# Bias rows shared with GpSimd as maxima, a two-product maximum as MLP activation, six of eight half batches turned by DMA, and a new issue order

## The chip, the cores and the metric

One core of one Trainium2 chip runs the kernel. Its engines are TensorE (PE for the matrix products, PEld for the loading of their stationary operand), VectorE (DVE), ScalarE (ACT), GpSimd (POOL) and SyncE (SP, which here only issues DMAs). The metric is the device time of one execution in microseconds, as the median of several executions.

## The reference, cut to what matters

```
# q, k, v: (4 batches, 8 heads, 576 positions, 64); hidden = 32; d_model 512; d_ff 2048
scores = q @ k^T / 8
psi_rel = log1p(|i - j|); psi_i = log1p(max(i, 1)); x = psi_rel / psi_i
h = max(x * w1 + b1, 0)            # 32 numbers for each pair (i, j)
bias = h @ w2                      # one number for each head and pair (i, j)
attn = softmax(scores + bias)      # with 1e-9 added to the sum
y = attn @ v                       # heads side by side: 2304 tokens x 512
h = y @ w_in                       # 2304 x 2048
g = max(h, 0) + alpha * min(h, 0)
out = g @ w_out                    # 2304 x 512
```

The weights of the MLP arrive as 64-bit floats and are put together from their two halves on the chip.

## The kernel before, in words

There is one program of some 14,700 instructions. Every step is recorded first as an operation with a sort key and a nominal duration (`Planner.op`), and some operations may run on either of two engines. `Planner.plan` then lays all of them out as a list schedule, from the table `ORDER` (a key for each part, offsets, and prices for the second engine of a choice), and the instructions are issued in that order on each engine. Each engine then runs its own list strictly in order, and semaphores hold it where an operand is missing. So the table, the nominal durations and the rules of the planner set what stands behind what on each engine and on SP's DMA queue.

The parts are these.

- **Bias net** (`bias_tile`, 36 tiles of 16 positions). A tile takes four *bias rows*: 128 partitions (4 positions x 32 hidden units) by 576, max(R + PSI, 0), each made by ACT (L473) or DVE (L470). PE multiplies the four by `w2b` (L482), ACT or DVE scales the result out of PSUM (L488, L491), and a DMA stores it in a scratch tensor in HBM.
- **MLP weights** (`weights`, 8 pieces `fp`). DVE puts the 64-bit numbers together (L650, L653: three instructions for 512 columns), the largest magnitude is found, ACT or POOL makes a rounded f16 half (L666, L667), and DVE the remainder in f16 (L393). The products then take three f16 passes in place of one in f32.
- **Queries and keys** (`qk_turn`). PE turns them (L560). Batch 0 keeps them in f32; batches 1 to 3 split them into two f16 halves.
- **Attention** (`unit`). Batch, half of the heads (`hf`, 4 heads), head pair and range of rows make a unit; a half batch is four units, two for rows 0 to 255 and two for rows 256 to 575. A unit works through *tiles* of 128 rows of one head (in the longer range one more tile holds the last 64 rows of both heads): scores on PE (L585 or L586), bias added and the maximum taken on DVE (L766), exponential and its sum on ACT (L769), sum plus 1e-9 and reciprocal on DVE (L772 or L774, L776). What follows has two forms, and `by_dma(b, hf)` chooses between them. In the f32 form POOL scales the tile by the reciprocal (L791), PE turns it in five 128 x 128 pieces (L800), ACT or DVE copies it out of PSUM (L810, L811), and PE multiplies by V in f32 (L829). In the DMA form POOL or ACT writes a scaled f16 half into a buffer `a16` (L781, L782), DVE writes the remainder beside it (L784), SP issues DMA transposes of the buffer (L787; the tile of 64 + 64 rows takes two), and PE multiplies by V in f16, three passes (L821). There are two `a16` buffers. The half batches (1,1), (2,0), (2,1) and (3,1) take the DMA form.
- **MLP** (`chunk`, 9 chunks of 256 tokens; `layer_pair`, 8 per chunk). PE makes 2 x 128 hidden units (L896, 24 matmuls) into the only buffer `H` in PSUM. ACT takes the positive and the negative part (L902, L903), DVE joins them with alpha (L905, twice), ACT or DVE rounds to f16 (L909), DVE or POOL makes the remainder (L910, L911), and PE adds into `O` (L917, 12 matmuls). A chunk needs all eight heads of its tokens.

```
def by_dma(b, hf):
    return (b, hf) in [tuple(i) for i in o_("dma", ((1, 1), (2, 0), (2, 1), (3, 1)))]
...
pl.op([("ACT", 790, on_act)] + [("DVE", 560, on_dve)], key, [t_R, t_T], [hb], tag="H")
...
A(lambda: nc.scalar.activation(g.t, hv(), AF.Relu, scale=sp), 700, ky, [hb, t_sig], [g])
A(lambda: nc.scalar.activation(nn.t, hv(), AF.Relu, scale=npt), 700, ky, [hb, t_sig], [nn])
```

## Time and profile before

| what | value |
|---|---|
| time, three runs | 746.77, 747.82 (median), 749.71 us |
| the profiled execution's own time | 744.54 us |
| its span, first to last instruction | 742.8 us |
| PE, DVE, ACT, POOL busy, share of the span | 93%, 70%, 60%, 16% |
| 16 DMA engines, SP's queue | 61.5% of their span |
| mean granted clock of TensorE | 0.992 |

The span is the time from the first instruction of any engine to the end of the last one; 1.7 us of the execution lie outside it. A busy share is an average over stages that differ: the first 161.5 us hold the bias net, the weights and the first attention of batch 0, the last 96.5 us the MLP alone.

### The profile page before, as it was taken

To read this page: it belongs to the slowest core of one execution; us is meant where nothing else is said; L and a number is where in the kernel's file an instruction comes from. 1 tells how busy PE (TensorE), PEld (TensorE's weight loads), DVE (VectorE), ACT (ScalarE), POOL (GpSimd) and SP (SyncE) were. 2 spreads that over 40 slices of the span, in tenths; PEclk is the share of its full clock that TensorE was granted. 3 is DMA by queue.
4 is the path that set the end of the run, shared out by engine and by line. 5 is a ranking of instruction groups with operands and counts; after the bars stand their busy time and mean duration, and the time that the engine had idled before them with its cause. 6 is when DMAs were issued, how large, how long until landed. Compare 5 with 4: busy or idle time off the path is not lost.

```text
span 742.8 us, 14670 instructions
## 1 busy us (share of the span) xinstructions
PE 687.5 (93%) x5425; PEld 429.9 (58%) x5425; DVE 521.3 (70%) x1281; ACT 447.0 (60%) x826; POOL 117.2 (16%) x149
## 2 busy tenths in 40 slices
PE   4888777689999989999999999999999999999997
PEld 1333333357566746665566666665686566666663
DVE  6898989898878877778678777666377666334342
ACT  5888988877655756666455666655576454132322
POOL 0000222323322222122011111122120011000000
PEclk9998999999999999999999999999999999999999
DMA  7999876525458256989898977966435867000000
GB/s 199 248 275 354 326 236 225 185 97 157 120 158 206 63 146 145 191 176 216 185 172 167 226 151 164 200 124 111 141 105 148 157 149 128 1 29 1 29 1 28
DMA packets 180998, 114.04 MB, mean 154 GB/s; under 512 B 157504, under 2 KB 157504, under 8 KB 180928
## 3 DMA queue, kind: packets, MB, share of 16 engines
q1 hardware_dynamic: 178624, 113.11, 61.5%
q8 instruction: 42, 0.69, 0.4%
q10 hardware_dynamic: 2304, 0.01, 0.2%
q14 instruction: 28, 0.23, 0.1%
HBM read 74.16 MB, written 15.34 MB: 120 GB/s over the span
## 4 chain that ended last, share of the span: by engine, by line
PE 62%; DMA 1%; DVE 1%; ACT 1%; issue 0%; SPq 0%; ACTq 0%; DVEq 0%
PE O L917 23%; PE H L896 22%; PE S L586 5%; PE A L821 4%; PE A L829 2%; PE S L800 2%; PE S L560 2%; DMA fg<-scr 1%; DVE fg L766 1%; PE O L800 0%; PE O L586 0%; ACT mg L877 0%; DMA out_dram<-mg 0%; PE A L455 0%; ACT fg L769 0%
## 5 line engine op out<-in xcount | busy, mean ns | idle before, releaser
L896 PE MATMUL H<-x,win 128*128 128x256 f16 x1728 | 200.7, 273 | 1.2 <-ACT mg L903 1.1
L917 PE MATMUL O<-wout,mg 128*128 128x512 f16 x864 | 199.1, 380 | 1.5 <-ACT at L810 0.8
L896 PEld LDWEIGHTS <-win 128*128 128x128 f16 x1728 | 166.9, 98 | 33.5 <-issue 7.2
L917 PEld LDWEIGHTS <-mg 128*128 128x128 f16 x864 | 81.6, 98 | 93.6 <-issue 5.7
L769 ACT ACTIVATE fg<-fg,st 128x576 f32<-128x576 f32 x144 | 110.3, 767 | 42.2 <-DVE st L766 38.6
L902 ACT ACTIVATE mg<-H,sm 128x512 f32<-128x512 f32 x72 | 49.4, 686 | 135.3 <-PE H L896 124.4
L905 DVE SCALAR_TENSOR_TENSOR mg<-mg,sm 128x256 f32<-128x256 f32 x144 | 68.5, 504 | 84.2 <-ACT mg L903 84.2
L766 DVE CUSTOM_DVE_ANT_0 fg<-S,fg 128x576 f32<-128x576 f32 x128 | 93.7, 751 | 33.6 <-PE S L586 29.3
L791 POOL TENSOR_SCALAR fg<-fg,st 128x576 f32<-128x576 f32 x72 | 62.5, 880 | 174.1 <-DVE st L776 61.8
L482 PE MATMUL S<-at,w2b 128*32 128x512 f32 (+1 forms) x448 | 63.1, 462 | 21.0 <-DVE at L470 10.2
L781 POOL TENSOR_SCALAR a<-fg,st 128x576 f16<-128x576 f32 x40 | 33.5, 838 | 221.9 <-DMA at<-a 51.1
L473 ACT ACTIVATE at<-cst 128x576 f32<-128x576 f32 x89 | 63.7, 765 | 5.7 <-DVE cst L433 5.7
L784 DVE SCALAR_TENSOR_TENSOR a<-fg,st,a 128x576 f16<-128x576 f32 x72 | 60.4, 844 | 4.0 <-POOL a L781 2.8
L482 PEld LDWEIGHTS S<-at,w2b 128*32 128x32 f32 x448 | 23.3, 117 | 60.1 <-issue 17.3
L586 PE MATMUL S<-qk 64*128 64x288 f16 (+1 forms) x654 | 51.3, 285 | 3.2 <-DVE st L766 2.4
L800 PE MATMUL S<-cst,fg 128*128 128x128 f32 x290 | 41.1, 281 | 9.7 <-POOL fg L791 7.0
L910 DVE TENSOR_TENSOR mg<-mg 128x512 f16<-128x512 f32 x68 | 47.2, 694 | 3.7 <-ACT mg L909 2.3
L903 ACT ACTIVATE mg<-H,sm 128x512 f32<-128x512 f32 x72 | 48.9, 680 | 0.1
L586 PEld LDWEIGHTS <-qk 64*128 64x128 f16 (+1 forms) x720 | 31.8, 97 | 25.9 <-issue 20.7
L829 PE MATMUL A<-at,five 128*64 128x320 f32 (+3 forms) x320 | 44.9, 415 | 0.6 <-DVE at L811 0.6
L800 PEld LDWEIGHTS S<-cst,fg 128*128 128x128 f32 x290 | 32.1, 142 | 17.3 <-POOL fg L791 8.5
L821 PE MATMUL A<-at,five 128*64 128x256 f16 (+3 forms) x480 | 34.3, 288 | 0.0
(136 smaller groups left out, 777.5 us busy)
## 6 DMA issues: line engine op xcount, KB each, us to landing
fg<-scr SPq DMA_DIRECT2D x64, 576.0 KB, 4.6
scr<-fg SPq DMA_DIRECT2D x36, 288.0 KB, 3.8
mg<-in_moe_w_in_dram SPq DMA_DIRECT2D x13, 512.0 KB, 5.5
mg<-in_moe_w_out_dram SPq DMA_DIRECT2D x12, 512.0 KB, 6.3
fg<-scr SPq DMA_DIRECT2D x32, 144.0 KB, 4.6
out_dram<-mg SPq DMA_DIRECT2D x18, 256.0 KB, 2.4
five<-in_q_dram SPq DMA_DIRECT2D x32, 128.0 KB, 4.0
five<-in_k_dram SPq DMA_DIRECT2D x32, 128.0 KB, 3.4
```

What stands on the lines that cost most here:

```text
L473: nc.scalar.activation(hb.t, R[:, lo:lo + S], AF.Relu, bias=PSI[:, g:g + 1], scale=1.0)
L482: nc.tensor.matmul(ps.t[32 * gl:32 * gl + 32, c:n], lhsT=w2b, rhs=hs[gl].t[:, c:n], start=True, stop=True)
L586: return [(lambda a, dst=dst, zq=zq, zk=zk, i=i: nc.tensor.matmul(dst(a), lhsT=tr16(qt)[at, 0, pr, zq, lo:lo + n], rhs=tr16(qt)[at, 1, pr, ...
L766: V(lambda x=x, sl=sl, st=st, ls=ls: nc.vector.tensor_tensor_reduce(out=in_halves(ls[x]()), in0=halves(sl[x].t), in1=in_halves(ls[x]()), s ...
L769: A(lambda x=x, st=st, ls=ls: nc.scalar.activation(ls[x](), ls[x](), AF.Exp, bias=st.t[:, x:x + 1], scale=-1.0, accum_out=st.t[:, 2 + x:3 ...
L784: V(lambda x=x, rec=rec, ls=ls, a16=a16: nc.vector.scalar_tensor_tensor(a16.t[:, 640:640 + S], ls[x](), rec(), a16.t[:, 0:S], op0=ALU.mult ...
L791: pl.op([("POOL", 850, lambda x=x, st=st, ls=ls: nc.gpsimd.tensor_scalar(ls[x](), ls[x](), st.t[:, 6 + x:7 + x], 1.0, op0=ALU.mult, op1=AL ...
L800: nc.tensor.transpose(t5()[:, c], ls[x]()[:, lo:lo + P], EYE)
L821: nc.tensor.matmul(ps.t[64 * hh:64 * hh + 64, 0:w], lhsT=v5[0:hi, zv, n, 2 * pr + hh, :], rhs=at16(at)[0:hi, 5 * za + n, 320 * hh:320 * hh ...
L896: nc.tensor.matmul(hb.t[:, f, :], lhsT=win[:, fp, zw, kb, P * f:P * f + P], rhs=x[:, zx, kb, :], start=(n == 0), stop=(n == 11))
L905: V(lambda f=f: nc.vector.scalar_tensor_tensor(g.t[:, 256 * f:256 * f + 256], nn.t[:, 256 * f:256 * f + 256], nal[:, 2 * fp + f:2 * fp + f ...
L917: nc.tensor.matmul(ob.t[:, t, :], lhsT=gg.t[:, zg, f, P * t:P * t + P], rhs=wout[:, fp, zw, f, :], start=(first and f == 0 and (zg, zw) == ...
```

## The change

Six edits come together.

1. A bias row may also be made by POOL, as max(R, -PSI), which is the old row less PSI. What is missing, w2b times PSI, is one number for each partition of the result, and is added when the tile leaves PSUM (`shift`, from a table `MASK` that is filled once, by a small product `beta_mm`). The chosen rows in the built program: 54 on ACT, 8 on DVE, 82 on POOL (before: 101, 43, 0).
2. The MLP's activation is the maximum of two products, both read from `H` in PSUM: ACT writes h times `cu`, DVE takes the maximum of that and h times `cs`, in two halves of 256 columns. Where alpha is over 1 the signs of `cs`, `cu` and of that row of w_out are turned, so w_out is scaled in two halves.
3. `by_dma` names six half batches: (1,0) and (3,0) are added.
4. The sum plus 1e-9 is one two-step instruction on DVE or POOL (63 of 80 on POOL).
5. The buffers `a16` are handed out in the order of the program.
6. The planner's nominal durations and the whole table `ORDER` are new.

```diff
-        return (b, hf) in [tuple(i) for i in o_("dma", ((1, 1), (2, 0), (2, 1), (3, 1)))]
+        return (b, hf) in [tuple(i) for i in o_("dma", ((1, 0), (1, 1), (2, 0), (2, 1), (3, 0), (3, 1)))]
...
+            def on_pool(g=g, hb=hb, lo=lo):
+                nc.gpsimd.tensor_scalar(hb.t, R[:, lo:lo + S], 3.0e38, npsi[:, g:g + 1], op0=ALU.min, op1=ALU.max)
+
+            made.append(pl.op([("ACT", 766, on_act), ("DVE", 532, on_dve), ("POOL", 840, on_pool)], key, [t_R, t_T, t_N], [hb], tag="H"))
...
+        def shift():
+            m = sum(1 << gl for gl in range(4) if made[gl].eng == "POOL")
+            return MASK[:, m:m + 1]
...
-            nc.scalar.activation(ev.t, ps.t[:, 0:S], AF.Copy, scale=EVI[:, t:t + 1])
+            nc.scalar.activation(ev.t, ps.t[:, 0:S], AF.Identity, scale=EVI[:, t:t + 1], bias=shift())
...
+                for f in range(2):
+                    sf = so[:, f:f + 1]
+                    on_act = lambda f=f, vw=vw, dst=dst, sf=sf: nc.scalar.activation(dst(0)[:, f], vw()[:, f], AF.Copy, scale=sf)
+                    on_pool = lambda f=f, vw=vw, dst=dst, sf=sf: nc.gpsimd.tensor_scalar(dst(0)[:, f], vw()[:, f], sf, 1.0, op0=ALU.mult, op1=ALU.mult)
...
-            V(add, 190, ky, [(st, 2 + x) for x in range(n)] + [t_eps], [(st, 4)])
+            pl.op([(nm, d, lambda e=e, st=st, n=n, up=up: e.tensor_scalar(st.t[:, 4:4 + n], st.t[:, 2:2 + n], 1e-9, up, op0=ALU.add, op1=ALU.mult))
+                   for nm, d, e in (("DVE", 175, nc.vector), ("POOL", 250, nc.gpsimd))], ky, [(st, 2 + x) for x in range(n)], [(st, 4)], tag="ep")
...
-        A(lambda: nc.scalar.activation(g.t, hv(), AF.Relu, scale=sp), 700, ky, [hb, t_sig], [g])
-        A(lambda: nc.scalar.activation(nn.t, hv(), AF.Relu, scale=npt), 700, ky, [hb, t_sig], [nn])
+            A(lambda f=f: nc.scalar.activation(gf(f), hb.t[:, f, :], AF.Copy, scale=cu[:, f:f + 1]), 455, ky, [hb, t_sig], [(g, f)])
+            V(lambda f=f: nc.vector.scalar_tensor_tensor(gf(f), hb.t[:, f, :], cs[:, f:f + 1], gf(f), op0=ALU.mult, op1=ALU.max),
+              475, ky, [hb, t_sig, (g, f)], [(g, f)])
...
-    "queued": 11774.3,
+    "share": 0.984,
+    "queued": 1592841.1,
```

On DVE the program now starts with the weights. These are its rows from the fourth on, before the change: the first numbers of the bias net (L427 to L434: w1, b1 and R, PSI, w2b) stand first, then two bias rows (L470).

```order
L414 MEMSET a_86 128x640
L414 MEMSET a_87 128x640
L427 TENSOR_REDUCE sm<-sm 128x1
L428 TENSOR_SCALAR sm<-sm 128x1
L429 RECIPROCAL sm<-sm 128x1
L430 TENSOR_TENSOR sm<-sm 128x1
L431 TENSOR_TENSOR sm<-sm 128x1
L432 TENSOR_SCALAR cst<-cst,sm 128x1148
L433 TENSOR_SCALAR cst<-cst,sm 128x144
L434 TENSOR_SCALAR w2b<-w2b,sm 128x32
L470 TENSOR_SCALAR at_84<-cst 128x576 x2
```

And DVE's rows of the same place in the changed kernel, where L669 and L672 put the weights together and L428 is the first row of the bias net.

```order
L416 MEMSET a_87 128x640
L416 MEMSET a_88 128x640
L669 TENSOR_SCALAR win<-mg 128x512
L672 SCALAR_TENSOR_TENSOR win<-mg,win 128x512 x2
L669 TENSOR_SCALAR win<-mg 128x512
L672 SCALAR_TENSOR_TENSOR win<-mg,win 128x512
L669 TENSOR_SCALAR wout<-mg 128x512
L672 SCALAR_TENSOR_TENSOR win<-mg,win 128x512
L672 SCALAR_TENSOR_TENSOR wout<-mg,wout 128x512
L669 TENSOR_SCALAR wout<-mg 128x512
L672 SCALAR_TENSOR_TENSOR wout<-mg,wout 128x512 x2
L676 TENSOR_REDUCE sm<-win 128x1
```

So the twelve weight instructions have moved ahead of the numbers that every bias row waits for. On POOL the bias net of the changed kernel looks as follows (L488 is a bias row, L692 and L698 are the rounded halves of the weights; `at_85` and `fg` hold bias rows).

```order
L698 TENSOR_SCALAR win<-win,sm 128x1024
L488 TENSOR_SCALAR at_85<-cst,npsi 128x576 x2
L692 TENSOR_SCALAR wout<-wout,sm 128x512
L488 TENSOR_SCALAR at_85<-cst,npsi 128x576 x13
L530 MEMSET five_78 64x256
L488 TENSOR_SCALAR at_85<-cst,npsi 128x576 x2
L698 TENSOR_SCALAR win<-five_79,sm 128x1024
L488 TENSOR_SCALAR at_85<-cst,npsi 128x576 x12
```

Before the change POOL had only the weights and the scaling of batch 0's tiles there; now 82 bias rows stand among them. On SP, where the first half batch of batch 1 is worked, the queue before the change holds loads alone (L739 and L752 read the bias back, L507 loads q, k and v).

```order
L739 DMA fg<-scr_105 128x1152
L507 DMA five_79<-in_q_dram 128x4x64
L507 DMA five_79<-in_q_dram 64x4x64
L739 DMA fg<-scr_105 128x1152
L752 DMA fg<-scr_106 64x576 x2
L739 DMA fg<-scr_105 128x1152 x2
L752 DMA fg<-scr_106 64x576 x2
```

The changed kernel has the transposes (L818) of that half batch among the same loads (L772, L785 and L526).

```order
L772 DMA fg<-scr_105 128x1152
L818 DMA_TRANSPOSE at_85<-a_87 128x10x128
L818 DMA_TRANSPOSE at_85<-a_88 128x10x128
L772 DMA fg<-scr_106 128x1152
L818 DMA_TRANSPOSE at_85<-a_87 128x10x128
L818 DMA_TRANSPOSE at_85<-a_88 128x10x128
L772 DMA fg<-scr_106 128x1152
L785 DMA fg<-scr_107 64x576 x2
L526 DMA five_77<-in_q_dram 128x4x64 x3
L818 DMA_TRANSPOSE at_84<-a_87 128x10x128
L818 DMA_TRANSPOSE at_84<-a_88 128x10x128
```

What moved is the turning of two half batches, from PE to this queue: 40 transposes more in the program, 120 in place of 80, and 180 PE matmuls of L800 fewer, 180 in place of 360.

## Rows read from the trace of the kernel before

**Rows 1.** The page, busy time, share of the span and instructions of each engine.
```profile
PE 687.5 (93%) x5425; PEld 429.9 (58%) x5425; DVE 521.3 (70%) x1281; ACT 447.0 (60%) x826; POOL 117.2 (16%) x149
```

**Rows 2.** Busy us by stretch: length, each engine (instructions), clock, DMA share, GB/s.
```profile
0.00:161.50 161.50, 118.70 (x888) 57.28 (x888) 138.44 (x326) 134.70 (x216) 29.49 (x35) 0.97 0.77 243
161.50:646.30 484.80, 477.32 (x3934) 312.83 (x3925) 350.26 (x890) 287.82 (x570) 87.69 (x114) 1.00 0.69 151
338.00:484.00 146.00, 144.09 (x1218) 92.76 (x1217) 110.05 (x276) 92.36 (x185) 22.56 (x28) 1.00 0.90 183
508.00:564.00 56.00, 55.96 (x514) 39.02 (x512) 35.18 (x90) 34.72 (x71) 11.89 (x16) 1.00 0.39 100
646.30:742.80 96.50, 91.48 (x616) 59.80 (x612) 32.56 (x66) 24.52 (x40) 0.00 (x0) 0.99 0.05 17
```

**Rows 3.** PE's waits in the first 161.5 us: us in total, times, longest.
```profile
PE S L482 <- DVE at L470: 10.2, 2, 9.5
PE S L482 <- ACT fg L488: 9.7, 12, 1.4
```

**Rows 4.** The chain that ended last, late stretches: start us, us, what.
```profile
386.21 2.28 PE A L821 x30
...
420.41 1.88 PE A L821 x30
...
525.83 2.46 PE A L829 x20
...
551.83 0.55 PE O L800 x5
...
553.02 0.74 PE S L800 x5
...
561.37 2.99 PE A L829 x20
...
572.35 2.70 PE O L917 x12
```

**Rows 5.** Instructions of a line: ns minimum/median/maximum, first and last start.
```profile
L470 DVE TENSOR_SCALAR at<-cst x41: 487/512/1290, 8.9 to 156.1; 128x576 f32<-128x576 f32 x41
L473 ACT ACTIVATE at<-cst x89: 759/765/777, 8.9 to 157.6; 128x576 f32<-128x576 f32 x89
L791 POOL TENSOR_SCALAR fg<-fg,st x72: 737/746/1705, 88.4 to 554.1; 128x576 f32<-128x576 f32 x72
L393 DVE SCALAR_TENSOR_TENSOR win<-win,sm x4: 1276/1278/1285, 30.3 to 126.9; 128x1024 f16<-128x1024 f32 x4
```

**Rows 6.** Timeline around 136 us, POOL and DVE: start us, us, what.
```profile
136.09 2.42 POOL L791 TENSOR_SCALAR fg<-fg,st 128x576 f32<-128x576 f32 x2
136.14 1.76 DVE L393 SCALAR_TENSOR_TENSOR win<-five,sm,win 128x1024 f16<-128x1024 f32 x1 [0.94 <-POOL win L667]
137.82 1.76 DVE L393 SCALAR_TENSOR_TENSOR wout<-five,sm,wout 128x1024 f16<-128x1024 f32 x1
```

**Rows 7.** Groups by form: busy us, mean ns, then idle before and its releaser.
```profile
L902 ACT ACTIVATE mg<-H,sm 128x512 f32<-128x512 f32 x72 | 49.4, 686 | 135.3 <-PE H L896 124.4 <-issue 4.9 <-DVE a L784 4.0
L905 DVE SCALAR_TENSOR_TENSOR mg<-mg,sm 128x256 f32<-128x256 f32 x144 | 68.5, 504 | 84.2 <-ACT mg L903 84.2
L849 DVE SCALAR_TENSOR_TENSOR x<-A,sm,x 128x256 f16<-128x256 f32 x10 | 4.8, 478 | 4.5 <-ACT x L847 4.5
L847 ACT ACTIVATE x<-A,sm 128x256 f16<-128x256 f32 x10 | 4.7, 470 | 5.6 <-PE A L829 5.6
```

**Rows 8.** The transposes of 338 to 484 us, their landing, the remainder, batch 1's first scores.
```profile
L787 SPq DMA_TRANSPOSE at<-a x40: 1207/1348/2508, 338.8 to 479.4; - x40
...
DMA to landing us min/median/max: 2.9/3.5/6.3
...
L784 DVE SCALAR_TENSOR_TENSOR a<-fg,st,a x72: 792/812/1717, 282.0 to 626.6; 128x576 f16<-128x576 f32 x72
...
L586 PE MATMUL S<-qk x654: 279/283/308, 224.8 to 615.5; 64*128 64x288 f16 x140, 64*64 64x288 f16 x24
```

More of the change, by code (lines that the diff above doesn't have):

```diff
@@ L434, in attention_then_moe, with beta_mm @@
     V(lambda: nc.vector.tensor_scalar(w2b, w2b, aw, None, op0=ALU.mult), SMALL, KEY0, [t_aw, t_w2], [t_w2])
-    V(lambda: nc.vector.tensor_scalar(nal, al, -1.0, None, op0=ALU.mult), SMALL, KEY0 + 500, [t_al], [t_nal])
+    V(lambda: nc.vector.tensor_scalar(sgn, al, 1.0, -2.0, op0=ALU.is_gt, op1=ALU.mult), SMALL, KEY0 + 500, [t_al], [t_nal])
+    V(lambda: nc.vector.tensor_scalar(sgn, sgn, 1.0, None, op0=ALU.add), SMALL, KEY0 + 500, [t_nal], [t_nal])
+    V(lambda: nc.vector.tensor_scalar(npsi, PSI, -1.0, None, op0=ALU.mult), dve2(NG), KEY0, [t_T], [t_N])
+    bps, beta, t_beta = Buf(cA), cols(1), ["beta"]
+    def beta_mm():
+        for gl in range(4):
+            nc.tensor.matmul(bps.t[32 * gl:32 * gl + 32, 0:1], lhsT=w2b, rhs=tb, start=True, stop=True)
+    PE(beta_mm, 300, KEY0, [t_w2, t_tb], [bps])
+    V(lambda: nc.vector.tensor_copy(beta, bps.t[:, 0:1]), SMALL, KEY0, [bps], [t_beta])
+    V(lambda: nc.vector.tensor_scalar(MASK, MASK, beta, None, op0=ALU.mult), SMALL, KEY0, [t_beta, t_c], [t_beta])
     def p2(ar, n, guard, key, tok):
@@ L884, in chunk, with layer_pair @@
             tt = 2 * c + t
-            DMA(lambda e, t=t, tt=tt: e.dma_start(out=out[tt * P:tt * P + P, :], in_=o[t].t), P * DM * 4, key + 0.02, [o[t]], [("out", tt)])
-    def layer_pair(c, fp, ob, first, last, sp, npt, t_sig, ky):
+            DMA(lambda e, t=t, tt=tt: e.dma_start(out=out[tt * P:tt * P + P, :], in_=o[t].t), P * DM * 3.4, key + 0.02, [o[t]], [("out", tt)])
+    def layer_pair(c, fp, ob, first, last, cs, cu, t_sig, ky):
         hb = Buf(cH)
```

126 lines of the change are left out of this document (65 added, 61 removed), and 34 rows, old and new, of the table ORDER.

## Prediction

> **What bounds the kernel now.** I read the page's busy shares first, to see which engine could be the bound at all: PE, with 687.5 of 742.8 us [rows 1]. Then I cut the span into stretches, because PE idles in one of them only: of the 55.3 us that it idles, 42.8 lie in the first 161.5 us and 7.5 in the 484.8 us after them [rows 2]. So there are two kernels in one. Up to 161.5 us PE waits; its longest waits there are for bias rows from DVE and for tiles that ACT scales [rows 3], and DVE and ACT are busy for 138.4 and 134.7 us of the stretch [rows 2]. After it PE is the bound nearly everywhere, and what counts is how long PE's own instructions take; I took those from the chain that ended last, in late stretches where PE never stops. The last view was the DMA side, since the change moves work there: between 338 and 484 us, full of transposes, the DMA share is 0.90, and between 508 and 564 us, without any, 0.39 [rows 2, 8].
>
> **PE's work: -28.6 us.** Each of the two half batches that change form is four units, two with 4 turned tiles and two with 5, so 36 turns of five matmuls go. In the chain a turn costs PE 0.55 us when another follows and 0.74 us at its longest [rows 4]; I take 0.65 between them: 36 x 0.65 = 23.4 us (19.8 to 26.6). The product with V goes from f32 to three f16 passes: 2.99 us become 2.28 in the units of 320 rows, and 2.46 become 1.88 in those of 256 [rows 4]. Four units of each kind give 4 x 0.71 + 4 x 0.58 = 5.2 us. Both sit where PE is full, so their whole length should come off, if what they are exchanged for keeps up.
>
> **The first stretch: -7 us.** Of 144 bias rows ACT loses 47, at 0.765 us 36 us of work, and DVE loses 35, at 0.512 us 17.9 us; POOL gets 82, at 0.746 us, the median of its nearest row L791, 61 us [rows 5]. POOL is busy for 29.5 of the 161.5 us [rows 2], so it has the room. DVE does not gain all of its 17.9: ahead of its first MLP row the new order puts five more softmax rows (some 0.8 us each, as the remainder rows, which also go over 576 columns [rows 8]), the remainders of two more weight blocks (1.28 each for 1024 columns [rows 5]) and two remainders of V that stood later (1280 columns, by the same row 1.6 each). That is some 10 us back, so DVE gains about 8.
>
> Against that stands contention. At 136 us POOL had two L791 rows to run while DVE ran two L393 rows: DVE's took 1.76 us each and not 1.28, POOL's pair 2.42 us and not 1.49 [rows 5, 6]. So each side lost about half a microsecond for each row that met the other. The Trainium skill (SBUF — State Buffer, "SBUF: two separate sides") says why this can be: VectorE and GpSimd share one pair of SBUF ports, a lock that one holds for a whole instruction, when the VectorE operation runs in a two-port mode or reads two SBUF tensors; the trace agrees in kind, and by that rule each of the 82 rows can stop DVE. From the rows: 82 x 0.48 = 39 us of DVE time if every one meets such a row, nothing if none does. The merging and splitting of weights is about half of DVE's work ahead of the MLP, and a meeting doesn't always cost the whole 0.48, so I take 15 us. DVE's work is then 7 us longer than before, against 23 us in which it now idles and the 36 us taken from ACT, part of which DVE waits for through PE. I make the stretch 2 us shorter (bounds: 25 shorter if the rows never meet, 15 longer if they meet in most cases). In the new order PE does 12 more score matmuls, two turns and a few small ones before its first MLP matmul, some 5 us. PE's idle time there falls by 2 + 5 = 7.
>
> The start is inside this: twelve weight instructions now stand ahead of the chain w1, R, w2b on DVE, so the first bias rows move from 8.9 us [rows 5] to some 14 us, and ACT, which begins with them, idles for these 5 us more; DVE does in that time what it would have done later.
>
> **Edits that I cost at nothing.** The activation: ACT's two rows of 0.686 become two of about 0.47 (the nearest row that reads 128x256 from PSUM), DVE's two of 0.504 become two of about 0.478 [rows 7]. That takes some 31 us from ACT and 4 from DVE, but PE doesn't wait for either in the MLP. Buffer H is held for 2 x 0.686 = 1.37 us before, and for 0.47 + 2 x 0.478 = 1.43 after; the 12 matmuls into O that lie between two fillings, 2.70 us [rows 4], cover both. Without that cover it would cost 0.06 us in each of 72 pairs, 4 us. The halves of w_out, the split sum of 1e-9 on POOL and the order of `a16` are instructions of engines that PE is not waiting for. The 1e-9 on POOL stands behind POOL's longer rows and holds the reciprocal on DVE; the other tile of the unit covers it, and without that it is up to 0.75 us in a tile's chain.
>
> **The denser transposes: +9 us.** The stretch from 338 to 484 us holds 40 transposes, those of four pairs of units, in 36.5 us a pair, of which the DMA engines are busy for 0.90 x 36.5 = 32.9 [rows 2, 8]. Set against the share of 0.39 without transposes, one of them takes (0.90 - 0.39) x 146 / 40 = 1.9 us of all DMA engines, so the 40 more add about 75 us to the DMA's work and 12 pairs in a row follow each other instead of 6, a pause and 2. Batch 1 began its scores at 224.8 us [rows 8]; with 2 us off the first stretch and 5 us less PE work between, that is some 217. With the tail of 96.5 us [rows 2] as before, a span of 716 leaves (716 - 217 - 96.5) / 12 = 33.5 us for a pair. The DMA needs 32.9 of them. It fits, narrowly. Two `a16` buffers also fit: rounded half 0.77 (as ACT's rows of 576), remainder 0.81, landing 3.5 [rows 5, 8], 5.1 us for each buffer and 2.6 for a tile, 23 us for the nine tiles of a pair; with the longest landing of 6.3 it would be 35. So there is no slack left for a clump of loads, and I let PE's idle time of 7.5 us in this part more than double, by 9 (bounds: 0 and 35, the latter with a pair at 36.5, the pace of before).
>
> **Sum.** 744.5 - 28.6 - 7 + 9 = 717.9 us for an execution like the profiled one. That one lies 3.3 us under the median of the runs shown, so I forecast 721.
>
> **The rivals.** (A) The forecast, PE's work comes off and little else changes: 721, its own range 710 to 733, chance 0.52. (B) Bias rows and weights do not meet much, and the first stretch shortens by the 25 us of its bound in place of 2: 721 - 23 = 698. For it: ACT and DVE lose 54 us between them. Against it: DVE was the fuller of the two and meets POOL more often. Chance 0.14. (C) The ports decide the first stretch, 15 us longer in place of 2 shorter: 721 + 17 = 738. For it: rows 6; against it: DVE's softmax rows, reductions and copies out of PSUM stand among the weights there too, and the trace shows no such row stretched beside POOL. Chance 0.13. The rule of the Trainium skill above (SBUF — State Buffer, "SBUF: two separate sides") is this rival's mechanism. (D) The transposes are the new bound. SP's queue is one list, the two `a16` buffers a ring, and ACT, which makes more of the rounded halves now (65 against 32), stands still when a buffer is not free, with exponentials behind it. The point from which it decides: at 33.5 us a pair PE is still the bound; at 36 us a pair the span is 217 + 12 x 36 + 96.5 = 745.5 and the change is worth nothing; at 38 us it is 769.5, some 774 as a median. For it: the DMA share. Against it: the pace of before was set by PE, which was busy for 144 of the 146 us. Chance 0.15, in two thirds of it slower. (E) The exchange saves PE little, since turns run while PE would wait anyway: about 745, chance 0.06; rows 2 speak against it, as PE hardly waits where they stand.
>
> **How the numbers follow.** A to C and a part of D lie under 744; what a measurement of this kernel can tell from no change is about 0.5%, 3.7 us. Faster: 0.52 + 0.14 + 0.13 and 0.04 of D and E, 0.83. Same: 0.06. Slower: 0.11, all D. The range leaves out the lower half of B and D's slow part: 700 to 745.
>
> **What would show it.** Right: PE busy near 659 us, 180 matmuls of the turn's line, PE idle about 36 us before its first MLP matmul and 15 to 20 up to the last product with V; POOL rows of the bias net at 0.75 us alone and over 1 us beside weight rows; transposes landing in 3.5 to 5 us. Wrong: PE idle for more than 40 us in the middle with ACT or POOL waiting for DMA (D), or a first MLP matmul before 145 us (B) or after 172 (C).

## The result, and the profile after

The changed kernel takes 755.8 us (median of 4 runs, 754.1 to 758.1) against 747.8 us (746.8 to 749.7) for the kernel before on the same chip: a ratio of 1.011, 95% interval 1.007 to 1.014. It is slower, where 721 us had been forecast. The profiled execution took 755.0 us.

The page's busy time of each engine, after (before: [rows 1]):

```profile
PE 679.5 (90%) x5333; PEld 412.4 (55%) x5333; DVE 532.5 (71%) x1232; ACT 399.6 (53%) x794; POOL 201.4 (27%) x269
```

PE is down by 8.0 us and not by 28.6, and its idle time, span less busy, went from 55.3 to 73.7 us. The stretches say where. After, busy time by stretch, columns as in [rows 2]: up to the first bias matmul, the bias net, from its last matmul to the first MLP matmul, from there to the last product with V, and the tail:

```profile
0.00:22.40 22.40, 6.77 (x21) 3.67 (x21) 14.79 (x36) 4.74 (x7) 1.67 (x6) 1.00 0.79 205
22.40:155.00 132.60, 95.44 (x666) 34.65 (x667) 108.39 (x204) 80.48 (x120) 110.15 (x106) 0.95 0.74 234
155.00:195.50 40.50, 36.24 (x252) 22.20 (x249) 35.83 (x105) 29.27 (x57) 20.53 (x29) 0.96 0.47 142
195.50:660.80 465.30, 454.42 (x3814) 294.47 (x3811) 341.01 (x823) 267.29 (x570) 69.07 (x129) 0.99 0.86 178
660.80:753.20 92.40, 86.67 (x594) 57.36 (x588) 32.47 (x66) 17.85 (x40) 0.00 (x0) 0.99 0.05 18
```

Two things are to be seen. From the first MLP matmul on little is lost: PE idles 10.9 us up to the last product with V, with the DMA engines busy for 0.86 of the time. The loss lies ahead of it: the first MLP matmul comes at 195.5 us, 34.0 us later than before [rows 2]. And in the bias net POOL, with 110.2 of 132.6 us, is now the busiest engine, with DVE close behind it.

The first MLP matmul is not the same point of the work in every kernel, so below I also use the first score matmul of batch 1, when all of batch 0 has its scores. Before it comes at 224.8 us [rows 8], after 6 MLP pairs; after, at 246.3 us, after 5 (a pair is (200.7 + 199.2) / 72 = 5.6 us of PE). The prediction had put it at 217. The 29.3 us between, and the pair, are 34.9 of the 37.1 us by which the profiled 755.0 us exceed the forecast's sum of 717.9. From there to the end: before 517.9 us, after 506.9, so 16.6 us came off with the pair counted, where 28.6 - 9 = 19.6 were forecast.

What the rows on GpSimd look like. Lines of POOL and DVE in the groups view after (columns as in [rows 7]):

```profile
L488 POOL TENSOR_SCALAR at<-cst,npsi 128x576 f32<-128x576 f32 x78 | 87.3, 1129 | 38.3 <-DVE npsi L438 18.0 <-PE S L497 12.4 <-PE O L497 6.6
...
L672 DVE SCALAR_TENSOR_TENSOR five<-mg,five 128x512 int32<-128x512 int32 x24 | 21.5, 926 | 0.0
...
L672 DVE SCALAR_TENSOR_TENSOR win<-mg,win 128x512 int32<-128x512 int32 x8 | 5.5, 685 | 0.1
...
L669 DVE TENSOR_SCALAR five<-mg 128x512 int32<-128x512 int32 x12 | 7.2, 616 | 0.0
```

A row takes 1.13 us in the mean and not the 0.746 of its model [rows 5]. One and the same merging instruction of the weights, L672, takes 0.685 us in the one group and 0.926 in the other. The timeline shows how both come about (start us, us, what; POOL, then DVE):

```profile
44.75 2.94 POOL L488 TENSOR_SCALAR at<-cst,npsi 128x576 f32<-128x576 f32 x2 [0.47 <-PE S L497]
49.00 1.46 POOL L488 TENSOR_SCALAR at<-cst,npsi 128x576 f32<-128x576 f32 x2 [1.30 <-PE S L497]
85.00 1.82 POOL L488 TENSOR_SCALAR at<-cst,npsi 128x576 f32<-128x576 f32 x1
...
45.41 3.42 DVE L672 SCALAR_TENSOR_TENSOR five<-mg,five 128x512 int32<-128x512 int32 x4
48.76 1.20 DVE L676 TENSOR_REDUCE sm<-five 128x1 f32<-128x1024 f32 x1
49.89 0.88 DVE L482 TENSOR_SCALAR at<-cst 128x576 f32<-128x576 f32 x1
...
84.94 0.75 DVE L394 SCALAR_TENSOR_TENSOR wout<-wout,sm 128x512 f16<-128x512 f32 x1 [0.51 <-POOL wout L692]
85.61 0.69 DVE L672 SCALAR_TENSOR_TENSOR win<-mg,win 128x512 int32<-128x512 int32 x1
86.21 0.89 DVE L669 TENSOR_SCALAR win<-mg 128x512 int32<-128x512 int32 x1
```

At 49.0 us two rows take 0.73 us each, the first of them wholly beside a reduction; the second meets DVE's own bias row L482, and that one takes 0.88 us and not 0.51 [rows 5]. At 44.75 two run beside four mergings: 1.47 us each, and the four lose 0.7 us together. The row at 85.0 finds the remainder L394 under way, then a merging, and ends 0.5 us after the merging, at 86.82; L669, which had begun meanwhile and takes 0.42 us elsewhere, takes 0.89 and ends behind the row. So, by these records, an instruction waits for the other engine's to end, and a row can wait for two in turn. Of the 82 rows, the 17 that meet neither L672 nor L394 nor one of the one-input instructions L669 and L482 take 0.733 to 0.746 us; the 61 that meet L672 or L394 take 1.26 us in the mean. The Trainium skill (SBUF — State Buffer, "SBUF: two separate sides") has this as an exclusive lock on a shared port pair, held for a whole instruction; the trace agrees, with the 1.82 us.

Who waits for whom in the bias net, after (us in total, times, longest):

```profile
PEld S L497 <- POOL at L488: 42.3, 40, 2.3
ACT fg L507 <- PE S L497: 40.4, 26, 3.6
...
PE S L497 <- POOL at L488: 14.8, 18, 1.4
```

PE waits for GpSimd's rows, and ACT, which scales the finished tiles, for PE. In part the wait is mutual: by the line of L488 above, GpSimd itself waited 12.4 + 6.6 us for row buffers that PE had still to read. PE also works longer on the same matmuls. PE timeline, before around 153 us and then after, around 114 us, one tile each:

```profile
152.88 1.18 PE L482 MATMUL S<-at,w2b 128*32 128x512 f32 x16
```
```profile
112.02 1.02 PE L497 MATMUL S<-at,w2b 128*32 128x512 f32 x2 [1.05 <-ACT fg L507]
113.36 1.05 PE L497 MATMUL S<-at,w2b 128*32 128x512 f32 x4 [0.33 <-POOL at L488]
115.56 1.16 PE L497 MATMUL S<-at,w2b 128*32 128x512 f32 x10 [1.15 <-POOL at L488]
```

The four rows of a tile go to four column groups of PE, and the sixteen records are eight of 512 columns and eight of 64. With all four rows there they overlap, and the tile takes 1.18 us. With the rows coming one after another the same sixteen take 1.02 + 1.05 + 1.16 = 3.2 us of busy time, in three pieces, so a late row also costs PE's own time. (The clock isn't the difference: a single matmul of 512 columns lasts 0.6 us in both tiles.) Before, 14 of the 36 tiles take under 1.3 us; after, 3 do. Busy time of single lines over the span (bias matmuls, turns, f16 and f32 products with V): before L482, L800, L821, L829,

```profile
0.00:161.50 161.50, 71.30 (x576) 26.00 (x576) 0.97 0.77 243
0.00:800.00 800.00, 49.71 (x360) 39.53 (x360) 0.99 0.58 143
0.00:800.00 800.00, 34.34 (x480) 24.03 (x480) 0.99 0.58 143
0.00:800.00 800.00, 44.93 (x320) 20.36 (x320) 0.99 0.58 143
```

and after L497, L831, L852, L860:

```profile
0.00:161.50 161.50, 82.14 (x576) 25.24 (x576) 0.96 0.73 224
0.00:800.00 800.00, 25.58 (x180) 19.76 (x180) 0.98 0.67 157
0.00:800.00 800.00, 51.50 (x720) 36.02 (x720) 0.98 0.67 157
0.00:800.00 800.00, 24.12 (x160) 10.76 (x160) 0.98 0.67 157
```

The turns lost 24.1 us and the products 3.7; the bias matmuls gave 10.8 back.

### The profile page after: what moved, and what is told of

The parts are those of the page before. It is cut to its first block, busy times and chain, and to the rows that moved or that the text cites. A ratio compares the mean times of both kernels' runs of the same rounds, so it can differ in the third digit from the quotient of the medians.

```text
span 753.2 us, 14646 instructions
## 1 busy us (share of the span) xinstructions
PE 679.5 (90%) x5333; PEld 412.4 (55%) x5333; DVE 532.5 (71%) x1232; ACT 399.6 (53%) x794; POOL 201.4 (27%) x269
## 4 chain that ended last, share of the span: by engine, by line
PE 69%; DVE 2%; ACT 1%; issue 1%; DMA 1%; POOL 0%; ACTq 0%; DVEq 0%; POOLq 0%
PE H L927 25%; PE O L946 24%; PE A L852 7%; PE S L605 6%; PE S L579 2%; PE A L860 2%; PE S L831 1%; DVE fg L799 1%; PE S L604 1%; DMA at<-a 1%; ACT mg L934 1%; DVE mg L935 1%; PE O L831 0%; PE O L604 0%; DVE a L815 0%
## 5 line engine op out<-in xcount | busy, mean ns | idle before, releaser
L927 PEld LDWEIGHTS <-win 128*128 128x128 f16 x1728 | 167.2, 98 | 36.4 <-issue 9.7
L935 DVE SCALAR_TENSOR_TENSOR mg<-H,sm,mg 128x256 f32<-128x256 f32 x144 | 65.2, 478 | 107.3 <-ACT mg L934 107.0
L934 ACT ACTIVATE mg<-H,sm 128x256 f32<-128x256 f32 x144 | 61.7, 469 | 121.8 <-PE H L927 121.3
L497 PE MATMUL S<-at,w2b 128*32 128x512 f32 (+1 forms) x496 | 78.1, 444 | 28.3 <-POOL at L488 14.8
L815 DVE SCALAR_TENSOR_TENSOR a<-fg,st,a 128x576 f16<-128x576 f32 x108 | 87.9, 818 | 14.9 <-ACT a L813 8.2
L488 POOL TENSOR_SCALAR at<-cst,npsi 128x576 f32<-128x576 f32 x78 | 87.3, 1129 | 38.3 <-DVE npsi L438 18.0
L812 POOL TENSOR_SCALAR a<-fg,st 128x576 f16<-128x576 f32 x43 | 34.1, 792 | 199.2 <-DMA at<-a 112.0
L497 PEld LDWEIGHTS S<-at,w2b 128*32 128x32 f32 x496 | 23.9, 114 | 81.1 <-POOL at L488 42.3
L805 POOL TENSOR_SCALAR st<-st 128x2 f32<-128x2 f32 (+1 forms) x63 | 20.1, 319 | 159.6 <-ACT fg L802 157.5
L813 ACT ACTIVATE a<-fg,st 128x576 f16<-128x576 f32 x65 | 50.0, 769 | 19.1 <-DMA at<-a 14.5
L852 PE MATMUL A<-at,five 128*64 128x256 f16 (+3 forms) x720 | 51.5, 288 | 0.0
L507 ACT ACTIVATE fg<-S,cst 128x576 f32<-128x576 f32 x34 | 28.1, 830 | 40.9 <-PE S L497 40.9
L852 PEld LDWEIGHTS <-five 128*64 128x64 f16 (+1 forms) x720 | 36.0, 109 | 15.7 <-issue 12.2
L485 ACT ACTIVATE at<-cst 128x576 f32<-128x576 f32 x45 | 32.9, 764 | 6.1 <-PE S L497 2.6
```

Of the source, the lines that this page charges most:

```text
L488: nc.gpsimd.tensor_scalar(hb.t, R[:, lo:lo + S], 3.0e38, npsi[:, g:g + 1], op0=ALU.min, op1=ALU.max)
L497: nc.tensor.matmul(ps.t[32 * gl:32 * gl + 32, c:n], lhsT=w2b, rhs=hs[gl].t[:, c:n], start=True, stop=True)
L813: ("ACT", 780, lambda x=x, rec=rec, ls=ls, a16=a16: nc.scalar.activation(a16.t[:, 0:S], ls[x](), AF.Copy, scale=rec()))],
L815: V(lambda x=x, rec=rec, ls=ls, a16=a16: nc.vector.scalar_tensor_tensor(a16.t[:, 640:640 + S], ls[x](), rec(), a16.t[:, 0:S], op0=ALU.mult ...
L852: nc.tensor.matmul(ps.t[64 * hh:64 * hh + 64, 0:w], lhsT=v5[0:hi, zv, n, 2 * pr + hh, :], rhs=at16(at)[0:hi, 5 * za + n, 320 * hh:320 * hh ...
L927: nc.tensor.matmul(hb.t[:, f, :], lhsT=win[:, fp, zw, kb, P * f:P * f + P], rhs=x[:, zx, kb, :], start=(n == 0), stop=(n == 11))
```

## The experiments

Theories: **contention** (rows on GpSimd and DVE's weight rows hold each other up, so GpSimd's pace sets the bias net), **order** (bias net and batch 0's attention now stand one after the other, with a later start), **DMA** (the transposes of two more half batches). A kernel called changed differs from the changed kernel by its diff alone, one called before from the kernel before. The median is of all executions, and the ratio is to executions of the kernel before on the same chip. The last four columns come from the one profiled execution of each kernel: times are those at which instructions of a kind first or last start, and the bias net goes from the first to the last of its matmuls over 512 columns.

| run | median us | ratio to before (95%) | bias net, us | first MLP matmul | batch 1's scores | from these to the end |
|---|---|---|---|---|---|---|
| before | 747.8 | 1 | 151.4 | 161.5 | 224.8 | 517.9 |
| changed | 755.8 | 1.007-1.014 | 132.1 | 195.5 | 246.3 | 506.9 |
| e1_reduce | 736.9 | 0.983-0.987 | 115.6 | 176.7 | 227.5 | 508.1 |
| e2_start | 761.3 | 1.016-1.021 | 135.0 | 202.0 | 252.8 | 510.0 |
| e3_half | 744.3 | 0.992-0.997 | 121.3 | 181.8 | 232.6 | 509.4 |
| f1_no_pool_rows | 746.0 | 0.996-1.001 | 122.4 | 182.6 | 233.4 | 509.9 |
| f2_quarter | 746.5 | 0.995-1.002 | 121.2 | 183.0 | 233.8 | 510.6 |
| e4_dma4 | 817.0 | 1.090-1.095 | 130.3 | 190.1 | 242.5 | 570.6 |
| g2_priced | 746.4 | 0.996-1.001 | 122.1 | 179.0 | 231.5 | 512.2 |
| g1_reordered | 756.9 | 1.008-1.019 | 153.5 | 184.6 | 236.7 | 518.0 |
| h1_old_start | 761.8 | 1.013-1.023 | 166.2 | 178.0 | 246.2 | 514.2 |
| h2_old_start_free | 763.0 | 1.015-1.032 | 161.7 | 167.2 | 246.3 | 512.9 |
| y1_one_half_batch | 743.2 | 0.991-0.998 | 154.2 | 164.6 | 227.9 | 513.5 |
| x3_identity | 750.3 | 0.998-1.005 | 156.7 | 166.9 | 230.2 | 517.9 |
| x4_maxima_in_before | 761.1 | 1.015-1.021 | 167.3 | 178.2 | 241.4 | 517.6 |
| x2_pool_in_before | 801.4 | 1.070-1.074 | 207.1 | 219.0 | 282.3 | 517.5 |

Six MLP pairs lie ahead of batch 1's scores in before, x, y and h, five in the others.

**e1_reduce: the merging instruction replaced by a reduction** (changed)

```diff
-  e.scalar_tensor_tensor(xi(), part(i), sc, xi(), op0=o0, op1=ALU.bitwise_or)
+  e.tensor_reduce(junk, xi().bitcast(F32), AX.X, ALU.max)
```

> The changed kernel in the same order, in which the 64 instructions of L672 on DVE (scalar_tensor_tensor, which puts the parts of a weight row together from two inputs in SBUF) are reductions over the same 512 columns, with one input. The weights are so not put together, and the MLP's output isn't the reference's. DVE keeps about its work; what goes is the second SBUF input beside GpSimd's bias rows. Contention (DVE and GpSimd stretch each other in SBUF, and GpSimd's rows, 1.13 us in the mean and not the 0.75 of the row that I priced them by, set the pace of the bias net): the mean of a bias row on GpSimd falls to 0.75-0.9, the stretch from the first to the last bias matmul from 132.6 to 100-112, the whole to 723-735. Order alone (the bias net and batch 0's attention now stand one after the other, and the start is later): the rows may get shorter, but the bias net stays within 5 us of 132.6 and the whole at 750-757. DMA (the turns by DMA are what costs): no change, 752-757.

Measured 736.9 us, 18.9 under the changed kernel; the bias net takes 115.6 us. Groups view of e1:

```profile
L488 POOL TENSOR_SCALAR at<-cst,npsi 128x576 f32<-128x576 f32 x78 | 72.3, 937 | 39.1 <-DVE npsi L438 18.2 <-PE S L497 13.1 <-PE O L497 6.5
...
L672 DVE TENSOR_REDUCE sm<-five 128x1 f32<-128x512 f32 x32 | 21.7, 679 | 0.3
...
L669 DVE TENSOR_SCALAR five<-mg 128x512 int32<-128x512 int32 x12 | 6.1, 529 | 0.0
...
L482 DVE TENSOR_SCALAR at<-cst 128x576 f32<-128x576 f32 x7 | 5.2, 756 | 4.0 <-PE O L497 2.3 <-PE S L497 1.7
```

With the order untouched and DVE's instruction hardly shorter (0.679 us), 18.8 us went at the first MLP matmul, and the reductions are not stretched. A reduction has one input and also writes one number for each partition in place of 512; which of the two matters can't be told here. Order alone had said 750 to 757 and DMA 752 to 757; both fall as the only cause. The three numbers lie just past the ranges that contention had given (0.75 to 0.9, 100 to 112, 723 to 735), and the trace shows what is left of it. The 41 rows that meet neither L394 nor L669 nor L482 take 0.73 to 0.76 us, the reductions beside them or not; the 21 that meet the two-input remainder L394 take 1.29 us in the mean. And the 20 that meet only the one-input instructions L669 and L482 take 0.94 us, up to 1.5; these two are stretched as well, to 0.53 and 0.76 us above, from 0.42 and 0.51. So it isn't only two-input instructions that collide.

**e3_half, f2_quarter, f1_no_pool_rows: fewer rows on GpSimd, same order** (changed; 41, 41 and none of the 82 left there)

```diff
+    rows = [o for o in ordered if o.tag == "H" and o.eng == "POOL"]
+    for o in rows[::2]:                        # e3_half; alts[0] is ACT, alts[1] DVE
+        o.eng, o.alt = "ACT", o.alts[0][2]
+    for i, o in enumerate(rows):               # f1_no_pool_rows (f2_quarter: i % 4 in (0, 2), by turns)
+        o.eng, o.alt = o.alts[i % 2][0], o.alts[i % 2][2]
```

> The changed kernel in the same order, with every second of the 82 bias rows that GpSimd makes put on ACT at the same place. Contention (GpSimd's pace bounds the bias net): GpSimd's busy time in that stretch falls from 110 us to about 60, ACT's rises from 80 to about 110, the bias net takes 110-118 us instead of 132.6, the whole 737-745. Order alone: the bias net takes what it took, since PE and the order bound it, or more, since ACT now has more: 754-775. DMA: no change, 752-757.

> The changed kernel in the same order, with a quarter of GpSimd's 82 bias rows put on ACT and a quarter on DVE, at the same places; 41 stay on GpSimd, as in the run with every second row on ACT (744.3 us). Contention: fewer rows for ACT than there (75 in place of 95, its busy time in the bias net 90 us in place of 105), and DVE has room because fewer rows meet it; the bias net takes 112-121 us and the whole 736-744. If DVE is what the bias net waits for once GpSimd's load is halved, it takes longer than with the rows on ACT: 745-752.

> The changed kernel in the same order, in which none of the 82 bias rows is left on GpSimd: every second goes to ACT and every second to DVE, at the same places. Contention (what the rows on GpSimd lose and make DVE lose is more than they save): ACT gets 41 x 0.765 = 31 us more, DVE 41 x 0.512 = 21 us more and gets back what the rows cost it (some 64 x 0.19 + 32 x 0.2 = 18 us at the weights), so DVE's work in the bias net stays near 110 us and ACT's comes to 111; the bias net takes 115-122 us instead of 132.6, the whole 737-745, as with half of the rows. Order alone, or GpSimd's rows as a real help (82 rows of work taken off ACT and DVE): the bias net gets longer, 135-150 us, the whole 757-775.

Measured 744.3, 746.5 and 746.0 us, all under the 752 or more that order and DMA had said. The first lies in contention's range for the whole, f1 1 us over it, and f2 in the range for the case that DVE is what the bias net waits for (DVE is busy there for 108.6 of 121.2 us). The bias nets miss contention's ranges, e3's 121.3 us by 3 (110 to 118), the others by less than 1; and f2's is no longer than e3's, as that case would have had it. Windows of the bias net, f1:

```profile
21.40:143.90 122.50, 92.59 (x666) 36.09 (x666) 106.23 (x242) 105.29 (x159) 23.15 (x24) 0.93 0.79 254
```

All 82 rows go back to ACT and DVE, and DVE's busy time is *lower* than in the changed kernel, 106.2 against 108.4 us, though it makes 41 rows more, 21 us of work: the rows on GpSimd had cost it some 23 us. The bias net is 9.7 us shorter than with them. That all three come out near 121 to 122 us suggests a second limit there, which is not GpSimd's pace; which one, no run shows.

**x2_pool_in_before, x4_maxima_in_before: GpSimd's rows alone, in the old order** (before; DVE's 43 rows move)

```diff
+    for o, on_pool in rows:
+        if o.eng == "DVE":
+            o.eng, o.alt = "POOL", on_pool
```
```
x2: nc.gpsimd.tensor_scalar(hb.t, R[...], PSI[...], 0.0, op0=ALU.add, op1=ALU.max)
x4: nc.gpsimd.tensor_scalar(hb.t, R[...], 3.0e38, PSI[...], op0=ALU.min, op1=ALU.max)
```

> The kernel before, in its own order, in which the 43 bias rows that DVE makes are made by GpSimd at the same places (the same sum and maximum, one instruction of 128x576 each); nothing else is changed. Contention: DVE loses 43 x 0.512 = 22 us of rows and gains back about 0.25 us of stretching for each GpSimd row (what 82 rows cost the weights in the changed kernel: some 20 us), 11 us; a row that takes 0.51 us on DVE takes over 1 us on GpSimd, and PE waits for it. The first MLP matmul at 157-168 us, the whole at 741-754. If GpSimd's rows are a plain help once the order is not the changed kernel's, the first MLP matmul comes at 145-155 us and the whole at 730-741.

> The kernel before, in its own order, in which the 43 bias rows that DVE makes are made by GpSimd at the same places, now in the changed kernel's form (a minimum with a constant and a maximum), which the run with sum and maximum (2.2 us a row) did not have; the missing sum isn't added later, so the output isn't the reference's. Contention: a row on GpSimd takes 1.0-1.2 us in the mean and not 0.75, the weights' two-input rows on DVE are stretched by 0.2-0.3 us a meeting; DVE loses 22 us of rows and gets some 11 back as stretching; PE waits for the longer rows. The first MLP matmul at 155-168 us, the whole at 740-753. Rows on GpSimd as a plain help outside the changed kernel's order: the first MLP matmul at 145-155 us, the whole at 730-740.

x2 took 801.4 us and says nothing of contention: its row costs 2.2 us by itself (last section). x4, with the changed kernel's form, took 761.1 us, over the end of what either theory had given (753 and 740), and so did its first MLP matmul (178.2, for 168 and 155). Windows of x4 up to that matmul, all and the line of the bias matmuls:

```profile
0.00:178.20 178.20, 131.21 (x889) 59.35 (x890) 132.25 (x290) 135.28 (x216) 68.89 (x78) 0.91 0.72 220
0.00:178.20 178.20, 82.26 (x576) 26.70 (x576) 0.91 0.72 220
```

Up to its first MLP matmul DVE is busy for 6.2 us less than in [rows 2], over the whole execution for 8.6 (512.7 us, for 521.3 in [rows 1]), though 43 rows of 0.512 us, 22 us, have gone: the rows on GpSimd gave DVE some 13 us of new busy time. And the first MLP matmul comes 16.7 us later. DVE's total was not what PE waited for. A bias row takes 0.94 us on GpSimd in the mean against 0.51 on DVE [rows 5]; PE needs four for a tile and waits for the last, its bias matmuls grow from 71.3 to 82.3 us as in the changed kernel, and its granted clock is 0.91 in this stretch against 0.97. What the row's own 0.74 us cost and what its stretching did, x4 doesn't separate.

**e2_start** (changed; the loads and instructions of the first weights and scales emitted first)

```diff
+    first = [o for o in ordered if o.part == "init" and o.rel < 100 and o.seq < beta_seq]
+    ordered = first + [o for o in ordered if o not in first]
```

> The changed kernel with the loads and instructions that set up the bias net's first weights and scales at the front of the order, as they stand in the kernel before; nothing else is changed. Late start (the first bias matmul at 22.4 us instead of 9.5): the first bias matmul at 9-14 us and the whole 8-13 us shorter, 742-747. Contention: the rows on GpSimd are as long as they were, the bias net keeps its 130 us or so; the whole is shorter by what the start gives and no more, the gap of 40 us between the last bias matmul and the first MLP matmul stays. If the start is hidden behind the loads of q and k, on which batch 0's scores wait, the whole stays at 752-757.

Measured 761.3 us: the edit missed. The first bias matmul came at 27.5 us and not earlier than 22.4, because PE's list has the turns of q and k ahead of it, and PE stood until 22.0 us, with the load of k as the last thing awaited. PE timeline of e2:

```profile
22.00 0.37 PE L465 MATMUL A<-cst,sm 128*1 128x128 f32 x1 [22.00 <-DMA five<-in_k_dram]
22.16 5.37 PE L580 MATMUL S<-cst,five 128*128 128x128 f32 x20
27.46 2.15 PE L498 MATMUL O<-at,w2b 128*32 128x512 f32 x16
```

It does show the price: a start 5.1 us later made the first MLP matmul 6.5 and the whole 5.5 us later. If an earlier start gave back as much, the changed kernel's, 12.9 us later than before, would be worth most of its 12.9 us; that is not shown, as no run brings back the start alone.

**e4_dma4** (changed; order made anew by the same rules)

```diff
-  ((1, 0), (1, 1), (2, 0), (2, 1), (3, 0), (3, 1))
+  ((1, 1), (2, 0), (2, 1), (3, 1))
```

> The changed kernel with four half batches turned by DMA, as before, and not six; the order is made by the same rules from the same tables. By the prediction's term for the exchange (about 28 us less PE work) the whole is 25-30 us longer, 778-786, and the first MLP matmul stays within 5 us of 195. If the transfers of the six are what made the change slower, the whole is at 748-757 or less, with less idle time of PE in the middle.

Measured 817.0 us, where DMA had said 757 at most; the first MLP matmul comes at 190.1 us, for 195.5 in the changed kernel. The 61 us are more than the exchange, though: PE is idle for 45.2 us after the first MLP matmul, for 16.6 in the changed kernel. I take it that the table of keys, not made for four, does that; so even the sign is weak evidence. What speaks against DMA is the table's last column, 506.9 us and not 517.9 with the transposes of six, for one pair more.

**y1_one_half_batch** (before; one half batch more, a16 in order, new keys for batch 3's parts and later chunks)

```diff
-  ((1, 1), (2, 0), (2, 1), (3, 1))
+  ((1, 1), (2, 0), (2, 1), (3, 0), (3, 1))
```

> The kernel before with one half batch more turned by DMA, (3,0), and nothing else of the change: the buffers a16 are handed out in the order of the program, and the keys of batch 3's parts and the later MLP chunks are new so that the order holds it; everything up to batch 2, the whole first stretch, stands as before. The prediction's term for one half batch is 28.6 / 2 = 14.3 us less PE work, less half of the 9 us for denser transposes: the whole 8 to 14 us under the kernel before, 734-740 us, with PE busy for some 673 us. If the exchange gives nothing of its own (PE's shorter work turns into idle time at the transposes): 744-752.

Measured 743.2 us, between the two ranges. From batch 1's scores on it is 4.4 us shorter, less than half of the 14.3 - 4.5 = 9.8 expected. Windows from there to the end, before and then y1, and y1's turns:

```profile
224.80:742.80 518.00, 506.93 (x4087) 331.84 (x4085) 330.80 (x809) 273.49 (x533) 70.22 (x93) 1.00 0.59 127
```
```profile
227.90:741.40 513.50, 498.53 (x4037) 323.18 (x4035) 343.02 (x833) 276.62 (x536) 52.25 (x70) 0.99 0.67 139
...
0.00:800.00 800.00, 37.85 (x270) 29.48 (x270) 0.98 0.62 150
```

The turns gave 11.9 us (11.7 forecast), the products with V nothing (2.6 forecast), PE as a whole 8.4, and 3.9 us of new idle time went against it (4.5 forecast). So the exchange is real, and here smaller than its sum. The first stretch, the same program as in before, took 3.1 us more here: such differences lie within what one profile can tell.

**x3_identity** (before)

```diff
-  nc.scalar.activation(ev.t, ps.t[:, 0:S], AF.Copy, scale=EVI[:, t:t + 1])
+  nc.scalar.activation(ev.t, ps.t[:, 0:S], AF.Identity, scale=EVI[:, t:t + 1], bias=eps[:, 0:1])
```

> The kernel before with ACT's scaling of a bias tile out of PSUM in the changed kernel's form (Identity with a bias operand; the bias is a column of 1e-9) instead of Copy; nothing else is changed. In the changed kernel this instruction takes 0.83 us, before 0.735, so 32 of them cost ACT 3 us more in a first stretch where ACT is busy for 134.7 of 161.5 us: the whole 0 to 4 us longer, 747-752. If the rest of the first stretch's loss lies in this edit (PE waits for these buffers), 755 or more.

750.3 us, not told apart from before; the instruction takes 0.83 us in place of 0.735, as in the changed kernel.

**g2_priced, g1_reordered, h1_old_start, h2_old_start_free: other orders** (changed). g2 gives the planner the measured price; g1 and h take all rows off GpSimd; h sets a key for each operation, those of the first part from the order of before.

```diff
-  [("ACT", 766, on_act), ("DVE", 532, on_dve), ("POOL", 840, on_pool)]
+  [("ACT", 766, on_act), ("DVE", 560, on_dve), ("POOL", 1150, on_pool)]      # g2_priced, with a new table
+  [("ACT", 766, on_act), ("DVE", 532, on_dve)]                              # g1_reordered, with a new table
+    for o, k, e in zip(pl.ops, KEYS, ENGS):                                 # h1 and h2
+        o.key = k
```

> The changed kernel with the planner's nominal duration of a bias row on GpSimd raised from 840 to 1150 ns, as measured, and on DVE from 532 to 560 ns, and a new table found for these by the planner's own rules: 59 rows on ACT, 23 on DVE, 62 on GpSimd. If the change lost because its order was made for rows of 840 ns that take 1130, the first MLP matmul comes at 160-172 us and the whole at 725-740, under both kernels. If contention can't be priced away by a longer nominal duration (DVE's own loss is in no nominal duration), the bias net still takes over 125 us, the first MLP matmul comes after 180 us and the whole at 742-756.

> The changed kernel without bias rows on GpSimd (they can only go to ACT or DVE), with a new table of keys, offsets and prices, found for that choice by the planner's own rules, starting from the keys of the kernel before for the first stretch. Order as the second cause (with no row on GpSimd the changed kernel's own order gave 746 us, its first MLP matmul at 182.6 us): a first stretch that is made for ACT and DVE gives back 10 to 20 us, the first MLP matmul at 163-173 us and the whole at 725-738. If contention is all there is, and what is left of the loss is work that the exchange and the activation add, the first MLP matmul stays at 176-185 us and the whole at 740-750.

> The changed kernel without bias rows on GpSimd, whose first part (bias net, weights, batch 0) is put in the order of the kernel before, operation by operation and with the engines chosen there (101 rows on ACT, 43 on DVE), and the rest in the order of the changed kernel, shifted per part. The exchange of the two half batches, the activation and the other edits stay. By the sum of the first scores of batch 1 (before at 224.8 us; the changed kernel at 246.3 us with one MLP pair less done, and 506.9 us from there to the end): if the loss lies in the first part alone, contention and order together, the first scores of batch 1 are back at 222-230 us and the whole is 728-738. If the exchange gives nothing of its own and what the changed kernel gained later was only work moved ahead, the whole is 744-752. Contention alone gives no help here: as the rows leave GpSimd it predicts what the run with no row on GpSimd gave, 746.

> As the run beside it (rows on ACT and DVE, first part in the order of the kernel before, the rest as in the changed kernel), with the engine free for the operations other than bias rows that may go to two. The same numbers: 726-738 if the loss lies in the first part alone, 744-752 if the exchange gives nothing of its own; the two kernels should lie within 6 us of each other, since they differ in the later order only.

Measured 746.4, 756.9, 761.8 and 763.0 us. g2's whole is within what contention gave if it can't be priced away (742 to 756), but its bias net, 122.1 us, and its first MLP matmul, 179.0, are a little better than that had said (over 125, after 180): with 62 rows still on GpSimd the measured price took 9.4 us off the changed kernel, and brought it level with before. The wholes of g1, h1 and h2 fall out of both expectations: no row is on GpSimd, h1 starts its bias net at 10.1 us, and yet batch 1's scores come 12 to 21 us later than before. Windows of h1 and, for the first of them, of before:

```profile
72.00:96.00 24.00, 15.02 (x98) 5.23 (x98) 18.26 (x49) 19.54 (x29) 1.49 (x1) 0.64 0.76 254
...
72.00:78.00 6.00, 3.98 (x29) 1.68 (x27) 5.40 (x12) 5.70 (x9) 0.00 (x0) 0.85 0.88 291
78.00:84.00 6.00, 3.12 (x23) 1.17 (x19) 5.68 (x18) 4.21 (x7) 1.49 (x1) 0.50 0.85 281
84.00:90.00 6.00, 2.27 (x19) 0.72 (x22) 3.29 (x10) 5.12 (x9) 0.00 (x0) 0.50 0.43 153
90.00:96.00 6.00, 5.64 (x34) 1.66 (x35) 3.89 (x10) 4.52 (x7) 0.00 (x0) 0.73 0.88 290
```
```profile
72.00:96.00 24.00, 18.56 (x125) 8.06 (x124) 22.18 (x57) 23.46 (x37) 3.96 (x4) 1.00 0.88 336
```

In h1 PE is busy for two thirds of its time from 72 to 78 us, the granted clock falls, and for 12 us it is at 0.50, the lower of its two levels (1.2 of 2.4 GHz); before stays at 1.00 there. PE, DVE and ACT all get less done in h1's 24 us than in before's, so they wait for each other more. What in these orders does it, and what the clock adds, isn't settled. They only show that my re-made orders were worse than the tuned one of before, and so say nothing on the order's share of the changed kernel's loss.

## Why the prediction was wrong

**PE's work: -28.6 us.** Right where it was counted: the turns lost 24.1 us (23.4 forecast), the products with V 3.7 (5.2). But PE's busy time fell by 8.0 only (679.5 us, where 659 had been named), for work that the sum did not touch grew: the bias matmuls by 10.8 us, for a reason that belongs to the next step, the turns of q and k by 3.1 and the MLP's matmuls by 2.3. Most of the 3.6 us that are left is overlap between the lines, which became less.

**The first stretch: -7 us.** This is the step that failed. It made the stretch 2 us shorter and took 7 us off PE's idle time in it. Measured, the first MLP matmul comes 34.0 us later: ahead of it PE idles 57.0 us and not 42.8, 14 us more, and works 19.7 us longer. The step read rows 6 rightly, that each side loses half a microsecond when a row meets a two-input weight instruction, and then charged it to DVE alone: 15 us of DVE time, against idle time that DVE had (f1 puts it at some 23). Three things are wrong in that. First, the price fell on GpSimd's rows too (0.746 forecast, 1.13 measured, 82 of them: 31 us), and GpSimd, thought to have the room, became the busiest engine of the stretch. Second, engines' totals were set against each other, while PE waits for the last of four rows; x4 shows DVE 6.2 us less busy and the stretch 16.7 us longer. Third, late rows make PE's own work on a tile longer.

By the sign that it named (a first MLP matmul after 172 us) this is rival C, and C had the mechanism. Two runs measure contention in this order, at the first MLP matmul: 18.8 us with the merging replaced (e1), 12.9 with the rows off GpSimd (f1). C's 17 us are of that size. They are about half of the 34; the other half is in no rival.

The start inside this step was put at some 14 us for the first rows; ACT's first came at 16.7 and the first bias matmul at 22.4, behind the turns of q and k, which I had not followed on PE's list. e2 prices a further delay about one to one.

What stays open is that other half: with no row on GpSimd (f1) the changed kernel's first MLP matmul still comes at 182.6 us, 21 later than before. Work moved ahead is some 6 us, near the 5 forecast (PE's busy time up to there in the changed kernel, 138.4 - 118.7, less the 10.8 and 3.1 above); the bias matmuls of f1 take 78.8 us, still 7.5 more than before with no row on GpSimd; the late start can be up to 13. How much of it is the start and how much the serial order, no run separates.

**Edits costed at nothing.** The activation: ACT's row takes 0.469 us and DVE's 0.478, as taken from [rows 7], and PE hardly waits for them:

```profile
PE S L605 <- DVE st L799: 3.2, 5, 1.1
PE O L946 <- DVE st L799: 2.5, 1, 2.5
...
PE H L927 <- DVE mg L935: 1.3, 3, 0.5
```

(PE's waits from the first MLP matmul to the end, after.) The bias eviction with its new operand, which I had not priced, is 0.095 us longer each, and x3 finds nothing that can be told from zero.

**The denser transposes: +9 us.** Right in kind: from batch 1's scores to the end PE idles 16.1 us after (506.9 - 490.8) and 11.1 before, 5 us more, and the 120 transposes land in 2.9/3.6/6.9 us (least, median, most), near [rows 8]. Rival D (the transposes as the bound) is refuted by this and by the last column of the table, rival B by the first stretch. Rival E (the exchange saves PE little) doesn't fit the 16.6 us of the changed kernel, in which the other edits also have a part; y1, the exchange of one half batch alone, got 4.4 of 9.8 and so goes half of the way to E.

**Two kernels just ahead of both.** e3_half, the changed kernel with every second of GpSimd's rows on ACT, and y1 are 0.5 to 0.6% faster than before, 744.3 and 743.2 us; both intervals exclude 1, neither by much.

## What to carry to other kernels

Work that is moved to an idle engine has to be priced beside what runs at the same time on the engine that it collides with, for both: where the trace shows two instructions stretching each other, multiply by the number of meetings and charge both lists, and ask first which of the two lists the next engine waits on. An engine that feeds another in groups is judged by the last member of the group, not by its total busy time. And where a change has a part that saves and a part that may cost, follow one milestone that both kernels reach with the same work done; here it put nearly the whole error into the first third.
